# Banded attention and three dense stages on one core: chaining the attention's loads in twos, splitting queries and keys, and moving the first dense weights

## The chip, the cores and the metric

The kernel runs on one core of a Trainium2 chip. The metric is device time in microseconds (us). The median of three runs of the kernel before is 586.44 us.

Names in this text: PE is TensorE's matmul, PEld its weight load, DVE is VectorE, ACT is ScalarE, POOL is GpSimd, SP is SyncE, whose queue issues nearly all loads. A line number such as L353 is one of the kernel before.

## The reference, cut to what matters

```python
# attention: batch 2, 8 heads, 768 positions, head size 64; n_sink = 4, window = 128
scores = q @ k.T / 8
keep = (key position < n_sink) | (0 <= query position - key position < window)
a = exp(where(keep, scores, -1e9) - max);  a = a / (sum(a) + 1e-9)
x = (a @ v), heads side by side               # 1536 tokens x 512
# dense stages
h = ((x @ w1) * (x @ w2)) @ w3                # 512 -> 1024 -> 1024
x2 = h @ w_out                                # 1024 -> 512
g = softplus(x2 @ w_in2);  out = g @ w_out2   # 512 -> 2048 -> 512
```

The weights arrive in 64-bit floats, everything else in 32-bit floats.

## The kernel before, in words

**Attention.** The 16 pairs of batch and head are worked off as eight pairs of heads. For each pair, six tiles of 128 queries go through these steps: `S` (PE, `score`, L362: scores of a tile for both heads), `M` (DVE, `mask`: adds the mask and takes the extreme), `E` (ACT, `exp`), then for a whole head `N` and `RC` (DVE: total and reciprocal) and `C` (POOL, `divide`, L407), then `T` (PE, `turn`, L420: transposes), `P` (DVE or ACT: copies out of PSUM), `PV` (PE, `pv`, L441, in two banks: first the products with `v`, then those with `vu`, the sinks and the 64 keys before), and `XH`/`XL` (ACT and DVE: the result as a high and a low part).

**Loads.** A pair's queries and keys are one tile, `qk` (792 KB, `load_qk`, L351, one DMA; for the first pair four DMAs), its values are another with two DMAs, `v` and `vu` (384 and 400 KB, `load_v`, L355). There are two buffers of each tile, so the `qk` of a pair waits for the last scores of the pair two before, and its `v` for the last `PV` of the pair two before. All of these loads are issued by SP, in one order, and SP stands still while the one at the head of its queue waits.

**Order.** The order of all steps of the attention is written out by `Plan.order` (L96). Each step has an engine, a modelled duration, the steps that it comes after and a rank; the planner takes, again and again, the ready step with the least earliest start plus 0.9 times its rank. `add` (L477) makes the rank from the place in the program plus 45 times an entry of `PUT_OFF` (L50). The `after` of a load in the plan sets only its place in the order; what it really waits for follows from the buffers. Before, the plan puts the `v` of a pair behind the scores of its third tile.

**Dense weights.** A weight of 512 KB (128 partitions of 512 64-bit numbers) is loaded as 16-bit pieces into one of three `raw` buffers (L184) and decoded into a high and a low part by `decode_steps` (L178): two operations on ACT, three on DVE, then two more on POOL (inside the attention) or DVE, and a copy on ACT. The two halves of the first dense weight, `w12_0_0` and `w12_0_1`, are steps `D` of the attention's plan (L561 to L571): their loads stand behind the `v` of the fifth pair. The halves of the later weights are written behind the attention and are ordered by the framework. The first dense matmul reads the second half, `w12_0_1`.

**Dense stages.** They follow the attention on PE. Every product is three matmuls (`mm3`, L162: high by high, high by low, low by high). The decoded halves stand in a ring of five, the raw ones in three buffers.

Of the kernel before, what the change touches and what calls it, by code (L numbers as in the profile page):

```python
# [19 lines left out]

P = 128
B, H, S, D = 2, 8, 768, 64
NT = B * S
DM = 512
FF = 1024
FF2 = 2048
QT = S // P
NSINK = 4
U = 64
NU = S // U  # L30
KU = NSINK + U
KR = 80
EW = KU + P
NPAIR = H // 2
NC = DM // P
NF = FF // P
NF2 = FF2 // P
CH = 512
# [9 lines left out]


PUT_OFF = dict(  # L50
    nw=-0.5, iota=-300.95, iotb=-45.02, val=-247.3, inw=-311.11, cur=102.51, snk=-47.1, km0=104.75, m_0=-95.95,
    inb=-325.17, prev=40.33, m_p=159.53, m_c=-271.18, m_1=-154.82, heat=19.73, q0=(157.18, 60.63),
    k0=(253.67, 361.64), v=(-113.46, -289.26, -139.37, -113.46, -113.46, -342.06),
    S=(65.96, 59.23, -40.01, 65.96, 65.96, 63.13), M=(-188.89, -61.46, -238.48, -169.62, -188.52, -188.6),
    E=(51.48, 54.22, 37.52, 48.22, 49.01, 50.81), N=(-98.0, 45.02, -53.12, -11.42, 55.33, 31.4),
    RC=(-236.66, -396.73, -301.38, -324.52, -237.63, -429.07),
    C=(26.92, -265.71, 18.67, -185.09, 17.21, -231.23), T=(66.85, 66.45, 62.14, 58.83, 71.95, 61.32),
    P=(-672.43, -474.71, -617.58, -470.82, -715.87, -434.29), PV=(72.94, 71.29, 69.88, 72.94, 72.94, 86.56),
    XH=(-316.3, 47.28, -280.25, -316.3, -316.3, 24.42), XL=(64.31, 59.48, 59.9, 64.31, 64.31, 18.36),
    qk=(55.01, 50.02, 55.01, 55.01, 55.01, -46.54), flag=333.92, D=(61.63, 49.66),  # L60
)

PVS = (
# [5 lines left out]
class Plan:  # L69
# [6 lines left out]
        DMA=dict(DVE=2000, ACT=2000, Pool=2000, PE=2000, DMA=0),  # L76
# [7 lines left out]
    @staticmethod  # L84
    def form(s):
        return {"S": "quarters", "PV": "columns"}.get(s["key"][0], "whole")

# [52 lines left out]
class Net:  # L140
# [192 lines left out]
    def attention(self, pool, psum):  # L333
        nc = self.nc
# [2 lines left out]

        bufs = dict(qk=2, v=2, e=4, st=4, pt=4)
        shape = dict(qk=[P, S + NU * KU], v=[P, QT + NU - 2, P], e=[P, QT, EW], st=[P, 3, QT], pt=[P, 2 * QT - 1, P])
        users = {}  # L340

        def buf(tag, h):

            if (tag, h) not in held:
                held[tag, h] = pool.tile(shape[tag], F32, tag=tag, name=f"{tag}{h}", bufs=bufs[tag])
            return held[tag, h]

        def free(tag, h):
            return users.get((tag, h - bufs[tag]), [])

        def load_qk(pair, cuts=((0, S + NU * KU),)):  # L351
            for a, b in cuts:
                nc.sync.dma_start(out=buf("qk", pair)[:, a:b], in_=self.qk[pair][:, a:b])  # L353

        def load_v(pair):  # L355
            nc.sync.dma_start(out=buf("v", pair)[:, 0:QT], in_=self.v[pair])
            nc.sync.dma_start(out=buf("v", pair)[0:KR, QT:], in_=self.vu[pair])

        def tile_columns(i):
            return slice(KU, EW) if i == 0 else slice(0, EW)  # L360
# [61 lines left out]
        def on_dve(h, g):  # L422

            return g == 2 or g == 1 and h % 2 == 0
# [52 lines left out]
        def add(kind, engine, ns, emit, *args, after=(), ring=None, off=0):  # L477

            put, at = PUT_OFF.get(kind, 0), list(args)
            if at and kind not in ("heat", "q0", "k0", "D"):  # L480
                ends = (B * NPAIR, kind in ("S", "PV", "XH", "XL", "qk", "v"))
                last = ends[0] - 1 if ends[1] else 2 * ends[0] - 2
                at[0] = at[0] % 2 + (2 if at[0] < (1 if ends[1] else 2) else 4 if at[0] >= last else 0)
            while type(put) is tuple:
                put = put[at.pop(0)]
            rank = len(plan.steps) + off + 45 * put
            plan.add((kind, *args), engine, ns, lambda: emit(*args), after, rank, ring)
# [11 lines left out]
        heat = psum.tile([P, CH], F32, tag="X0", name="heat", bufs=1)  # L499
# [11 lines left out]
        for j in range(2):  # L511
            q, k = hq[j], slice(S + hc[j].start, S + hc[j].stop)
            last = [("k0", 0)] if j else []
            add("q0", "DMA", 1200 if j else 700, lambda j, q=q: load_qk(0, [(q.start, q.stop)]), j, after=last)
            add("k0", "DMA", 1300 if j else 730, lambda j, k=k: load_qk(0, [(k.start, k.stop)]), j, after=[("q0", j)])

        scores = [(pair, i) for pair in range(H * B // 2) for i in range(QT)]
        for pair in range(B * H // 2):
            heads = (2 * pair, 2 * pair + 1)
            if pair:  # L520

                add("qk", "DMA", 2900 if pair > 1 else 3300, load_qk, pair, after=free("qk", pair) + [("v", 0) if pair > 1 else ("k0", 1)])
            add("v", "DMA", 2900, load_v, pair, after=free("v", pair) + [("S", pair, 2) if pair else ("qk", 1)])
            for i in range(QT):
                n = scores.index((pair, i))
                need = [("qk", pair)] if pair else [(x, j) for x in ("q0", "k0") for j in range(1 + (i > 2))]
                need += [("S", *scores[n - 1])] if n else [("heat", j) for j in range(38)]
                need += [("heat", j) for j in range(38 if n == 3 else 48, 48 if n == 3 else 64)] if n in (3, 6) else []
                need += [("M", 2 * scores[n - 2][0] + par, scores[n - 2][1]) for par in range(2)] if n > 1 else []
                add("S", "PE", 346 if i else 200, score, pair, i, after=need)  # L530
                m = [] if pair else [(x,) for x in (("m_0",), ("m_1",), ("m_p",))[min(i, 2)]]
                for h in heads:
                    add("M", "DVE", 283 if i else 212, mask, h, i, after=[("S", pair, i), *free("e", h), *m])
                    add("E", "ACT", 442 if i else 385, exp, h, i, after=[("M", h, i)])
            users["qk", pair] = [("S", pair, i) for i in range(QT)]
            for h in heads:
                add("N", "DVE", 78, total, h, after=[("E", h, i) for i in range(QT)])
                add("RC", "DVE", 104, inverse, h, after=[("N", h)])
                for i in range(QT):
                    add("C", "Pool", 403 if i else 346, divide, h, i, after=[("RC", h)])  # L540
            for h in heads:
                for g in range(3):
                    need = [("C", h, 2 * g), ("C", h, 2 * g + 1)]
                    add("T", "PE", 440 if g else 330, turn, h, g, after=need, ring=("PT", ("P", h, g)))
                    to = ("DVE", 602) if on_dve(h, g) else ("ACT", 480 if g else 375)
                    add("P", *to, turned, h, g, after=[("T", h, g), *free("pt", h)])
                users["e", h] = [("T", h, g) for g in range(3)]
            for bank in range(2):
                need = [("P", h, g) for h in heads for g in ((2,) if bank else (0, 1))] + [("v", pair)]
                need += [("XL", pair - 1, bank)] if pair else []  # L550
                add("PV", "PE", 853 if bank else 1493, pv, pair, bank, after=need)
            users["v", pair] = [("PV", pair, b) for b in range(2)]
            for h in heads:
                users["pt", h] = users["v", pair]
            for bank in range(2):
                n = S - CH if bank else CH
                add("XH", "ACT", 50 + 0.84 * n, x_hi, pair, bank, after=[("PV", pair, bank)])
                add("XL", "DVE", 61 + 1.055 * n, x_lo, pair, bank, after=[("XH", pair, bank)])
            if pair == 1:
                h = 3  # L560
                add("flag", "DVE", 780, lambda: self.window_flag(pool), after=[("val",)], off=6)  # L561
                self.first = [
                    self.ring.tile([P, 2, CH], FR, tag="u", name=f"u_w12_0_{j}", bufs=5) for j in range(2)
                ]
                for j, u in enumerate(self.first):
                    need = [("v", 4)]
                    for k, (engine, ns, emit) in enumerate(
                        self.decode_steps(self.w12[0][:, j, :], u[:, 0, :], u[:, 1, :], f"w12_0_{j}", pool_too=True)
                    ):
                        add("D", engine, ns, lambda j, k, emit=emit: emit(), j, k, after=need)  # L570
                        need = [("D", j, k)]  # L571

        for s in plan.order(dict(PE=600, DVE=500, ACT=2000, Pool=500, DMA=1700)):
# [394 lines left out]
```

## Time and profile before

| | us |
|---|---|
| runs | 586.44, 589.6, 586.17 |
| median of the runs | 586.44 |
| profiled execution | 587.49 |
| its span, first to last instruction | 585.2 |
| mean granted clock of TensorE | 0.994 |
| first dense matmul | 77.92 from the span's start |
| data loaded and stored | 54.51 MB, mean 93 GB/s |

The page gives for each engine the busy time, its share of the span and the number of instructions. [...] The waits view and the brackets of the timeline name what ended an idle time; "issue" there is an idle time that ended without any event that the profile shows. The DMA view lists the packets of each queue in a stretch: q1 holds the loads, q8 and q14 the code of the engines.

### The profile page before, as it was taken

The page shows a single profiled execution, that of the slowest core. Times are in us where ns is not written, and L with a number is a line of the kernel's source. Part 1 is how long each engine was busy: PE and PEld are TensorE (multiplying, and loading weights), DVE is VectorE, ACT ScalarE, POOL GpSimd, SP SyncE. Part 2 cuts the span into 40 slices and gives each one's busy share as a digit, 9 for nine tenths or more (in the row PEclk, how much of TensorE's full clock was granted, in tenths as well). Part 3 has the DMA queues.
Part 4 walks back from the last instruction along what each step waited for, and adds up shares of the span by engine and source line. Part 5 has one row for each costly group of instructions (what it writes and reads, how often), then busy time and mean ns, then how long its engine had stood idle before and what let it go on. Part 6 is the DMA issues. An engine that isn't in the chain of part 4 may idle for free.

```text
span 585.2 us, 9853 instructions
## 1 busy us (share of the span) xinstructions
PE 575.0 (98%) x3728; PEld 475.5 (81%) x3728; DVE 432.0 (74%) x906; ACT 348.0 (59%) x712; POOL 77.2 (13%) x162
## 2 busy tenths in 40 slices
PE   8999899999999999999999999999999999999996
PEld 7788788888888788888888788888888888888885
DVE  6889699989998976775998899845644544654553
ACT  6899877667665664554566778544444344444352
POOL 3566620000000000000000110110110111011010
PEclk9999899999999999999999999999999999999998
DMA  7759434545543542441644031000200000200002
GB/s 234 212 179 266 150 111 151 146 134 161 159 148 109 155 134 72 144 143 37 183 143 141 21 124 38 0 1 0 73 0 2 1 2 0 73 0 1 0 1 78
DMA packets 15800, 54.51 MB, mean 93 GB/s; under 512 B 1920, under 2 KB 2432, under 8 KB 15744
## 3 DMA queue, kind: packets, MB, share of 16 engines
q1 hardware_dynamic: 15456, 53.27, 29.5%
q8 instruction: 31, 0.51, 0.4%
q10 hardware_dynamic: 288, 0.52, 0.2%
q14 instruction: 25, 0.20, 0.1%
HBM read 50.64 MB, written 3.15 MB: 92 GB/s over the span
## 4 chain that ended last, share of the span: by engine, by line
PE 64%; DMA 4%; DVE 4%; ACT 3%; issue 0%; POOL 0%; ACTq 0%; SPq 0%; DVEq 0%
PE h L166 7%; PE h L164 7%; PE h L165 7%; PE ox L164 4%; PE ox L166 4%; PE o L166 4%; PE x2p L164 4%; PE x2p L165 4%; PE o L164 4%; PE o L165 4%; PE ox L165 4%; PE x2p L166 4%; PE ab L166 3%; PE ab L165 3%; PE ab L164 3%; DMA raw_w<-w3t 3%
## 5 line engine op out<-in xcount | busy, mean ns | idle before, releaser
L709 POOL TENSOR_SCALAR spu<-spa 128x512 f32<-128x512 f32 (+1 forms) x49 | 30.7, 626 | 462.9 <-ACT spa L708 462.9
L149 DVE TENSOR_TENSOR gl<-spl,gh 128x512 fp32r<-128x512 f32 x47 | 32.7, 696 | 76.8 <-ACT gh L723 76.6
L707 ACT ACTIVATE spa<-h 128x512 f32<-128x512 f32 (+1 forms) x49 | 28.8, 587 | 88.4 <-PE h L166 88.2
L166 PE MATMUL ab<-x,u_w 128*128 128x512 f32 x192 | 74.8, 390 | 0.3 <-DVE u_w L149 0.3
L164 PE MATMUL ab<-x,u_w 128*128 128x512 f32 x192 | 74.8, 390 | 0.0
L165 PE MATMUL ab<-x,u_w 128*128 128x512 f32 x192 | 74.7, 389 | 0.0
L164 PE MATMUL h<-y,w4h 128*128 128x512 f32 x192 | 74.7, 389 | 0.0
L166 PE MATMUL h<-y,w4l 128*128 128x512 f32 x192 | 74.7, 389 | 0.0
L165 PE MATMUL h<-y,w4h 128*128 128x512 f32 x192 | 74.7, 389 | 0.0
L191 ACT ACTIVATE dt_w<-raw_w 128x512 bf16<-128x512 bf16 x64 | 42.4, 669 | 52.2 <-DVE dr_w L208 11.2
L199 DVE SCALAR_TENSOR_TENSOR dc_w<-raw_w,dt_w 128x512 uint16<-128x512 uint16 x64 | 44.5, 701 | 10.8 <-ACT dt_w L194 9.7
L194 ACT ACTIVATE dt_w<-dt_w,rebias 128x512 uint16<-128x512 uint16 x64 | 45.8, 722 | 1.4
L714 DVE SCALAR_TENSOR_TENSOR spu<-spu,spa 128x512 f32<-128x512 f32 (+1 forms) x49 | 33.3, 680 | 17.5 <-ACT spl L712 17.4
L393 ACT ACTIVATE e<-e,st 128x196 f32<-128x196 f32 (+1 forms) x96 | 42.2, 446 | 1.9 <-DVE st L386 1.9
L407 POOL TENSOR_SCALAR e<-e,st 128x196 f32<-128x196 f32 (+1 forms) x96 | 39.7, 437 | 26.6 <-ACT e L393 15.5
L166 PEld LDWEIGHTS ab<-x,u_w 128*128 128x128 f32 x192 | 36.0, 188 | 8.2 <-DVE u_w L149 0.7
L164 PEld LDWEIGHTS ab<-x,u_w 128*128 128x128 f32 x192 | 36.0, 188 | 7.6
L165 PEld LDWEIGHTS h<-y,w4h 128*128 128x128 f32 x192 | 36.1, 188 | 7.6
L166 PEld LDWEIGHTS h<-y,w4l 128*128 128x128 f32 x192 | 36.0, 188 | 7.5
L164 PEld LDWEIGHTS h<-y,w4h 128*128 128x128 f32 x192 | 36.0, 188 | 7.4
L165 PEld LDWEIGHTS ab<-x,u_w 128*128 128x128 f32 x192 | 36.0, 188 | 7.3
L712 ACT ACTIVATE spl<-spu 128x512 f32<-128x512 f32 (+1 forms) x49 | 30.5, 624 | 19.2 <-POOL spu L709 18.5
(127 smaller groups left out, 1311.3 us busy)
## 6 DMA issues: line engine op xcount, KB each, us to landing
raw_w<-w4d SPq DMA_DIRECT2D x32, 511.8 KB, 4.1
raw_w<-w SPq DMA_DIRECT2D x16, 511.8 KB, 4.5
raw_w<-w3t SPq DMA_DIRECT2D x16, 511.8 KB, 3.8
qk<-qk SPq DMA_DIRECT2D x7, 792.0 KB, 6.1
raw_wo<-wod SPq DMA_DIRECT2D x8, 511.8 KB, 3.7
v<-vu SPq DMA_DIRECT2D x8, 400.0 KB, 6.5
v<-v SPq DMA_DIRECT2D x8, 384.0 KB, 5.3
out<-os SPq DMA_DIRECT2D x10, 256.0 KB, 2.2
```

Of the source, the lines that this page charges most:

```text
L149: return engine.tensor_tensor(out=lo, in0=x, in1=hi.bitcast(F32), op=ALU.subtract)
L164: nc.tensor.matmul(ps, lhs[0], rhs[0], start=start, stop=False)
L165: nc.tensor.matmul(ps, lhs[0], rhs[1], start=False, stop=False)
L166: nc.tensor.matmul(ps, lhs[1], rhs[0], start=False, stop=stop)
L191: return nc.scalar.activation(t.bitcast(BF), x["top"].bitcast(BF), AF.Abs)
L194: return nc.scalar.activation(x["t"], x["t"], AF.Relu, bias=self.rebias[:, 0:1], scale=8.0)
L199: nc.vector.scalar_tensor_tensor(out=c, in0=x["top"], scalar=0x8000, in1=t, op0=ALU.bitwise_and, op1=ALU.bitwise_or)
L393: nc.scalar.activation(e, e, AF.Exp, bias=st[:, 0, i : i + 1], scale=-1.0, accum_out=st[:, 1, i : i + 1])
L407: nc.gpsimd.tensor_scalar(out=e, in0=e, scalar1=buf("st", h)[:, 2, i : i + 1], scalar2=1.0, op0=ALU.mult, op1=ALU.mult)
L709: nc.gpsimd.tensor_scalar(out=u[:, c], in0=a[:, c], scalar1=1.0, scalar2=1.0, op0=ALU.add, op1=ALU.mult)
L712: nc.scalar.activation(l[:, c], u[:, c], AF.Ln)
L714: nc.vector.scalar_tensor_tensor(out=u[:, c], in0=u[:, c], scalar=1.0, in1=a[:, c], op0=ALU.subtract, op1=ALU.subtract)
```

## The change

Each load of the attention's pairs, from the third pair on, and the load of each of the two first dense halves gets a dependence on the load issued two places before it in the list `loads`, with a real wait (`DependencyClass.Sync`). The loads of the first two pairs go on the list without a wait. `qk` of the pairs after the first is cut into queries (384 KB) and keys (408 KB), two DMAs. In the plan, a `v` comes after the scores of its pair's first tile (second pair: after the third pair's `qk`), the two dense halves come after the `v` of the third and of the fourth pair in place of the fifth, and loads are modelled with 3300 ns. All entries of `PUT_OFF` are new.

```diff
@@ PUT_OFF
-    nw=-0.5, iota=-300.95, iotb=-45.02, val=-247.3, inw=-311.11, cur=102.51, ...
+    nw=-0.5, iota=-317.65, iotb=-43.77, val=-256.36, inw=-267.68, cur=70.88, ...
...
-    qk=(55.01, 50.02, 55.01, 55.01, 55.01, -46.54), flag=333.92, D=(61.63, 49.66),
+    qk=(-10.74, -6.13, -10.74, -10.74, -10.74, -96.08), flag=262.31, D=(60.89, 63.1),
@@ attention
-        users = {}
+        users, loads = {}, []
...
-        def load_qk(pair, cuts=((0, S + NU * KU),)):
+        def behind(load, pair):
+            if pair > 1:
+                self.tc.add_manual_dep(
+                    load.ins, loads[-2].ins.name,
+                    mybir.DependencyInfo(mybir.DependencyClass.Sync, mybir.DependencyReason.DATA), reason="two loads",
+                )
+            loads.append(load)
+
+        def load_qk(pair, cuts=((0, S), (S, S + NU * KU))):
             for a, b in cuts:
-                nc.sync.dma_start(out=buf("qk", pair)[:, a:b], in_=self.qk[pair][:, a:b])
+                behind(nc.sync.dma_start(out=buf("qk", pair)[:, a:b], in_=self.qk[pair][:, a:b]), pair)
 
         def load_v(pair):
-            nc.sync.dma_start(out=buf("v", pair)[:, 0:QT], in_=self.v[pair])
-            nc.sync.dma_start(out=buf("v", pair)[0:KR, QT:], in_=self.vu[pair])
+            behind(nc.sync.dma_start(out=buf("v", pair)[:, 0:QT], in_=self.v[pair]), pair)
+            behind(nc.sync.dma_start(out=buf("v", pair)[0:KR, QT:], in_=self.vu[pair]), pair)
...
-                add("qk", "DMA", 2900 if pair > 1 else 3300, load_qk, pair, after=free("qk", pair) + [("v", 0) if pair > 1 else ("k0", 1)])
-            add("v", "DMA", 2900, load_v, pair, after=free("v", pair) + [("S", pair, 2) if pair else ("qk", 1)])
+                add("qk", "DMA", 3300, load_qk, pair, after=free("qk", pair) + [("v", 0) if pair > 1 else ("k0", 1)])
+            add("v", "DMA", 3300, load_v, pair, after=free("v", pair) + [("S", pair, 0) if pair > 1 else ("qk", pair + 1)])
...
-                    need = [("v", 4)]
+                    need = [("v", 2 + j)]
...
-                        add("D", engine, ns, lambda j, k, emit=emit: emit(), j, k, after=need)
+                        add("D", engine, ns, lambda j, k, emit=emit: behind(emit(), 2) if k == 0 else emit(), j, k, after=need)
```

## Rows read from the trace of the kernel before

**Rows 1.** The page, part 1: busy us, share of the span, instructions.
```profile
PE 575.0 (98%) x3728; PEld 475.5 (81%) x3728; DVE 432.0 (74%) x906; ACT 348.0 (59%) x712; POOL 77.2 (13%) x162
```

**Rows 2.** Windows: stretch, length, PE PEld DVE ACT POOL busy, PEclk, DMA share, GB/s.
```profile
16.00:18.00 2.00, 1.43 (x35) 1.05 (x36) 1.97 (x9) 2.00 (x11) 0.67 (x2) 1.00 0.89 219
...
60.00:62.00 2.00, 0.47 (x12) 0.38 (x14) 0.82 (x6) 0.94 (x6) 2.00 (x6) 1.00 1.02 397
...
63.10:66.50 3.40, 3.40 (x42) 2.61 (x41) 2.69 (x16) 2.72 (x12) 0.70 (x2) 0.50 0.04 12
...
sum 80.00, PE 75.54 PEld 63.10 DVE 63.91 ACT 67.36 POOL 46.58; mean PE 1.89 PEld 1.58 DVE 1.60 ACT 1.68 POOL 1.16
```

**Rows 3.** Timeline of PE: start us, us, what, count, idle before and its end.
```profile
17.11 0.79 PE L379 MATMUL s<-qk 64*64 64x128 f32 x24 [0.57 <-DMA qk<-qk]
...
31.37 0.79 PE L379 MATMUL s<-qk 64*64 64x128 f32 x24
...
45.47 0.90 PE L379 MATMUL s<-qk 64*64 64x68 f32 x32
...
58.40 1.62 PE L456 MATMUL xt<-pt,v 128*64 128x64 f32 x37
61.55 0.45 PE L456 MATMUL xt<-pt,v 68*64 68x64 f32 x7 [1.53 <-issue]
...
64.19 1.58 PE L379 MATMUL s<-qk 64*64 64x68 f32 x32
...
77.92 0.50 PE L164 MATMUL ab<-x,u_w 128*128 128x512 f32 x1
```

**Rows 4.** Waits: engine, line, releaser, us in total, times, longest.
```profile
PE xt L456 <- issue: 1.7, 2, 1.5
...
PE s L507 <- DVE idle L914: 1.0, 1, 1.0
...
PEld pt L420 <- issue: 1.6, 8, 0.3
```

**Rows 5.** Windows between the two "issue" waits; the page's instruction queue.
```profile
20.40:61.50 41.10, 39.55 (x886) 33.14 (x886) 36.16 (x169) 38.41 (x152) 26.70 (x62) 1.00 0.76 223
...
q8 instruction: 31, 0.51, 0.4%
```

**Rows 6.** DMA queues, 53.9 to 58.9 and 58.9 to 60.3: packets, MB, share.
```profile
q1 hardware_dynamic: 366, 1.27, 101.6%
...
q8 instruction: 1, 0.02, 5.4%
```

**Rows 7.** Timeline of SP's queue: start us, us, line, load, count.
```profile
24.58 6.36 SPq L353 DMA_DIRECT2D qk<-qk  x2
...
52.72 0.33 SPq L356 DMA_DIRECT2D v<-v  x1
...
53.57 1.38 SPq L187 DMA_DIRECT2D raw_w<-w  x3
```

**Rows 8.** Issues from 24.5, 34, 53.9, 74 us: count, KB each, us to landing.
```profile
qk<-qk SPq DMA_DIRECT2D x1, 792.0 KB, 5.6
...
v<-v SPq DMA_DIRECT2D x1, 384.0 KB, 3.4
...
raw_w<-w SPq DMA_DIRECT2D x3, 511.8 KB, 9.0
...
raw_wo<-wod SPq DMA_DIRECT2D x1, 511.8 KB, 3.7
```

**Rows 9.** Timeline of DVE, decode of the second dense half.
```profile
72.41 0.81 DVE L199 SCALAR_TENSOR_TENSOR dc_w<-raw_w,dt_w 128x512 uint16<-128x512 uint16 x1
...
73.70 0.79 DVE L208 SCALAR_TENSOR_TENSOR dr_w<-raw_w,dt_w 128x512 f32<-128x512 uint32 x1
```

**Rows 10.** Dense stage, 78 to 204 us: window, and PE's only wait there.
```profile
78.00:204.00 126.00, 125.82 (x554) 103.79 (x554) 117.45 (x221) 84.09 (x144) 0.00 (x0) 1.00 0.46 141
...
PE ab L166 <- DVE u_w L149: 0.3, 1, 0.3
```

More of the change, by code (lines that the diff above doesn't have):

```diff
@@ L50 @@
 PUT_OFF = dict(
[L51 to L59, printed above, removed]
-    qk=(55.01, 50.02, 55.01, 55.01, 55.01, -46.54), flag=333.92, D=(61.63, 49.66),
+    nw=-0.5, iota=-317.65, iotb=-43.77, val=-256.36, inw=-267.68, cur=70.88, snk=-194.23, km0=13.82, m_0=-40.84,
+    inb=-272.77, prev=42.97, m_p=72.04, m_c=-258.34, m_1=-102.89, heat=29.6, q0=(95.24, 95.41),
+    k0=(198.35, 341.02), v=(-254.09, -273.51, -124.74, -254.09, -254.09, -315.44),
+    S=(78.14, 70.61, -90.97, 78.14, 78.14, 72.39), M=(-126.74, 0.02, -182.88, -137.85, -183.95, -184.15),
+    E=(57.87, 58.44, -44.22, 57.55, 57.69, 61.31), N=(-232.84, -113.11, -108.47, -70.53, -51.12, -82.6),
+    RC=(-49.11, -236.6, -182.17, -214.72, -83.93, -241.17), C=(22.8, -309.04, 28.65, -135.73, 32.93, -305.93),
+    T=(76.97, 74.12, 72.61, 67.98, 80.4, 79.23), P=(-715.08, -387.66, -481.84, -445.05, -588.27, -305.45),
+    PV=(83.23, 86.96, 82.61, 83.23, 83.23, 92.27), XH=(-268.48, 58.65, -320.52, -268.48, -268.48, 125.99),
+    XL=(70.77, 69.43, 83.14, 70.77, 70.77, 68.26), qk=(-10.74, -6.13, -10.74, -10.74, -10.74, -96.08),
+    flag=262.31, D=(60.89, 63.1),
 )
```

## Prediction

> **What bounds the kernel now.** I read the page first. PE is busy for 98% of the span [rows 1], so a change of loads can only pay where PE stands still or runs at its low clock. [...] At 17.11 the scores of the third pair start 0.57 us late, on a `qk` load. At 61.55 the second product of the sixth pair (`pv`) goes on after 1.53 us idle, ended by "issue": nothing that the profile names released it. The list of waits has 1.7 us of that kind on PE, in two waits, and eight short ones, 1.6 us in all, on the weight loads of the turns [rows 4].
>
> What is "issue" here? The stall lies inside one `pv`: 37 of its 44 matmuls run, then 7 after the stall, so no new tile starts there. The counts give the place. From the "issue" wait at 20.4 us to that of 61.5 us, PE took in 886 matmuls and 886 weight loads, 1,772 instructions, and semaphore instructions that the view leaves out [rows 5]. The page has an instruction queue with 31 packets and 0.51 MB: 16.5 KB a packet, and 7,456 matmuls and weight loads divided by 31 are 240 a packet [rows 1, 5]. 1,772 is about seven of these (253 each). I read this as seven blocks of code, with both stalls at the seam of a block. The DMA view says when the block came: from 53.9 to 58.9 us the data queue takes 101.6% of the 16 engines and no instruction packet is among its 366; the next one comes between 58.9 and 60.3 [rows 6]. What filled the queue is on SP's timeline: `v` and `vu` of the seventh pair at 52.72, and three dense loads from 53.57 [rows 7], which took 9.0 us to land where one alone takes 3.7 [rows 8]. So PE ran out of code because its next block stood behind the loads in flight, and the fall of the clock followed the stall.
>
> [...]
>
> **The change part by part.**
> 1. *Each load of pairs 2 to 7, and the two first dense halves, wait for the load two places ahead.* At most two chained loads are then in flight, about 0.8 to 0.9 MB, where the four of 53 us and those before them put over 2 MB in front of a code block. Removed: the idle 1.53 us. Bounds: 0 (stall kept) and 1.7 (both PE waits of this kind). I take 1.5, since even one 792 KB `qk` alone in flight has left at most 0.3 us waits on the weight loads [rows 4].
> 2. *The low clock after the stall.* 3.4 us at half clock do 1.7 us of work [rows 2]; 32 score matmuls took 1.58 us there against 0.90 at 45.47 [rows 3]. If the stall goes, 1.7 us go; the 0.57 us stall at 17 us was followed by no fall (1.00 in its window). Bounds 0 and 1.7; I take 1.7.
> 3. *The wait itself, on SP's queue.* Behind a waiting load stand all later loads, and PE waits for these. Two in flight, each landing in 3.4 us like a `v` alone [rows 8], give one load every 1.7 us, so 6.8 us for the four of a pair; the pairs follow each other every 7.1 us (scores of the third at 17.11, of the fifth at 31.37 [rows 3]). It just fits. The pair that also carries a dense half needs 3.7 / 2 = 1.9 us more, 8.7 us, and lags by up to 1.6. The `qk` of the fifth pair was issued at 24.58 and landed 5.6 us later, 1.2 us ahead of its use [rows 3, 7, 8]. Bounds 0 and +1.6; I take 0, nearest to a pair without a dense half, of which there are more.
> 4. *`qk` in two loads.* Seven more issues on SP of about 0.4 us (0.33 us each on its timeline), in a queue that mostly waits. At the third pair, where `qk` was already 0.57 us late [rows 3], its first half now waits for the `v` of the first pair, but no longer shares with the loads behind it. Bounds −0.6 and +0.7 (as much again); I take 0.
> [...]
> 5. *The dense halves earlier.* The second half's decode stood in the tail: its two long VectorE operations at 72.41 and 73.70 [rows 9], followed by GpSimd's, just ahead of the first dense matmul at 77.92 that reads it. Had only the stall gone, that decode would have been the next thing late. Moved up, its 1.6 us of VectorE lie beside the middle pairs. Cost there: between 0 and 1.6; I take 0, since VectorE's score work waits for PE.
> 6. *The new weights of the planner* reorder steps on all engines; the trace cannot show the new order. PE's idle time in the first 80 us other than its first wait (1.0) and the stall is 1.9 us (80 less 75.5 busy, less 2.5 [rows 2, 4]), so a better order gives 1.9 at most; I allow the same as a loss and take 0.
> 7. *Hand-over.* From 78 to 204 us PE is busy 125.8 of 126, VectorE 117.5, and PE waits once, 0.3 us, for a decoded weight [rows 10]. The dense stage thus has no spare on either side. Bounds: all of the gain passes, or none. I take all: VectorE and ScalarE leave the attention earlier by the same 3.2 us, and VectorE has 1.6 us less to do in its tail.
>
> Sum: −1.5 − 1.7 = −3.2 us. The profiled execution took 587.49 us around a span of 585.2, 1.05 above the median of 586.44; its sum is 584.3, and against the median I predict **583.2**.
>
> **Rivals.**
> *The stall stays or comes back elsewhere.* Only chained loads wait. The two dense loads that stood right behind the second half at 53.57 (three in one row [rows 7]) are outside the attention and not chained; if they follow its new place at once, four loads of 0.4 to 0.5 MB are again in flight among the turns. For it: they were issued within 1.4 us of the first. Against: two chained loads beside them, not four. Half the stall and no fall of the clock gives 585; all of it 586.4. Centre 585.8. The stall also stays, at 586.4, if its cause is no missing code. [...]
> *Given back at 204 us.* If the decode chain does not move, PE's one wait grows from 0.3 to 3.5 us [rows 10] and the time is 586.4; half gives 584.8. For it: VectorE at 93%. Against: point 7.
> *A `qk` load late, on the slower side.* Place: fifth pair, 31.37. If the first dense half stands ahead of this `qk`, it is issued at about 24.6, and the second half of `qk` waits for it to land. Landing in 3.7 us gives 24.6 + 3.7 + 3.4 = 31.7, 0.3 us late. Beyond 31.37 every microsecond is PE's. With 7.4 us (between 3.7 alone and 9.0 in company [rows 8]) PE idles 4.0 us and then runs at half clock, another 1.7: −3.2 + 5.7 = +2.5, about 589. At 9.0 us it is +4.1, 590.5. It ends slower than before if the dense half takes more than 4.9 us to land: `qk` is then 1.5 us late, as long as the stall that the fall of the clock followed, and 1.5 + 1.7 eat the 3.2. Against: the chain keeps company small.
>
> **How the numbers follow.** Forecast 0.55 (581.3 to 585.1: a gain of 3.2 that points 3 to 6 move by 1.9 either way), stall back 0.13, given back 0.17, `qk` late 0.15. From 581.2 to 587.6 the range takes in the forecast, both middle rivals, and the mild end of the last. About 1%, 5.9 us, is what a measurement can tell from no change: faster than 580.6 needs nearly all idle time of the attention besides, 0.05; slower than 592.3 needs two late loads, 0.04; within, 0.91.
>
> **What would show it.** Right: no "issue" wait of over 0.5 us on PE before the dense stage; the clock at 1.00 from 60 to 70 us; the first dense matmul at about 74.7 instead of 77.92; PE's wait near 201 us not over 0.5. Wrong: an idle stretch of PE ended by a `qk` load (the third rival); an instruction packet again missing from a long stretch of full queue (the first); a first dense matmul that is early with a wait of microseconds near 200 us (the second).

## The result, and the profile after

| | before | after |
|---|---|---|
| median, us (6 runs each) | 585.79 | 592.3 |
| lowest to highest, us | 583.44 to 589.6 | 591.12 to 592.82 |
| ratio, 95% interval | 1 | 1.0109 (1.0073 to 1.0145) |
| profiled execution, its span, us | 587.49, 585.2 | 592.09, 589.3 |
| mean granted clock | 0.994 | 0.993 |
| first dense matmul of the unbroken dense stage, us | 77.92 | 83.00 |

The changed kernel is slower by 6.4 us (4.3 to 8.5); I had predicted 583.2 and at most 587.6. Its code stands a few lines lower: `score` is L387, `turn` L428, `pv` L464, the loads of `qk`, `v` and `vu` L361, L364 and L365; the dense load keeps L187. Everything in this section is of the changed kernel.

The page has the same work as before [rows 1]:

```profile
PE 575.5 (98%) x3728; PEld 475.9 (81%) x3728; DVE 431.3 (73%) x906; ACT 348.6 (59%) x712; POOL 76.2 (13%) x162
```

The windows answer [rows 2, 10] (columns as there; the stretches come from several answers):

```profile
50.00:52.00 2.00, 0.00 (x0) 0.00 (x0) 0.44 (x3) 2.00 (x9) 1.09 (x3) 0.95 0.37 138
52.00:54.00 2.00, 0.23 (x4) 0.26 (x8) 0.00 (x0) 1.04 (x6) 1.30 (x4) 0.50 0.19 68
...
51.81:58.63 6.82, 4.86 (x60) 4.14 (x62) 2.98 (x11) 1.23 (x6) 1.49 (x4) 0.50 0.59 180
...
sum 82.00, PE 73.75 PEld 61.04 DVE 61.30 ACT 66.22 POOL 45.92; mean PE 1.80 PEld 1.49 DVE 1.50 ACT 1.62 POOL 1.12
...
83.00:209.00 126.00, 126.00 (x560) 104.34 (x557) 119.81 (x225) 85.52 (x144) 0.00 (x0) 1.00 0.45 147
```

From 60 to 62 us nothing stands still any more. In its place PE does nothing from 50 to 52 us and little from 52 to 54, and its granted clock is 0.50 from 51.8 to 58.6; 1.00 and 0.50 are the only two levels in this trace and in that of the kernel before. The timeline and the waits of PE (columns as in [rows 3, 4]) give the names:

```profile
13.64 0.49 PE L387 MATMUL s<-qk 64*64 64x68 f32 x9 [0.49 <-issue]
...
16.88 0.79 PE L387 MATMUL s<-qk 64*64 64x128 f32 x24 [0.34 <-DMA qk<-qk]
...
21.08 0.57 PE L464 MATMUL xt<-pt,v 68*64 68x64 f32 x11 [1.06 <-issue]
...
32.40 0.79 PE L387 MATMUL s<-qk 64*64 64x128 f32 x24
...
53.77 1.36 PE L387 MATMUL s<-qk 64*64 64x128 f32 x24 [4.49 <-DMA qk<-qk]
...
65.85 2.73 PE L464 MATMUL xt<-pt,v 128*64 128x64 f32 x72
...
83.00 0.50 PE L164 MATMUL ab<-x,u_w 128*128 128x512 f32 x1
```

```profile
PE s L387 <- DMA qk<-qk: 4.8, 2, 4.5
PE xt L464 <- issue: 1.1, 1, 1.1
...
PE s L387 <- issue: 0.5, 1, 0.5
```

The scores of the seventh pair wait 4.49 us for `qk`. The bank of 72 matmuls at 65.85 runs whole, where before one was cut by the stall. But two stalls that end with "issue", 0.49 and 1.06 us, have come at 13.64 and 21.08.

Why was that `qk` late? The chain of waits, read backwards from 53.77 (start us, us, what), leads through three loads, the second and the third each held by the one before:

```profile
36.85 4.52 DMA v<-v
...
41.38 3.79 DMA raw_w<-w
...
45.19 8.44 DMA qk<-qk
...
53.77 1.36 PE s L387 x24
```

The first of them was held too: by the waits of SP's queue it stood 1.8 us for the first half of the sixth pair's `qk`, two places ahead, and went at 36.85.

And SP's queue shows what stood between them (as [rows 7]); below it the landing times of those issues (as [rows 8]):

```profile
36.85 0.33 SPq L364 DMA_DIRECT2D v<-v  x1
37.83 0.33 SPq L365 DMA_DIRECT2D v<-vu  x1
41.38 1.96 SPq L187 DMA_DIRECT2D raw_w<-w  x3
43.44 2.08 SPq L361 DMA_DIRECT2D qk<-qk  x2
```

```profile
raw_w<-w SPq DMA_DIRECT2D x3, 511.8 KB, 7.4
qk<-qk SPq DMA_DIRECT2D x1, 408.0 KB, 8.4
...
qk<-qk SPq DMA_DIRECT2D x1, 384.0 KB, 9.2
```

The row of three dense loads is the point. The first is the second dense half, which the chain holds until the fourth pair's `v` has landed at 41.37. The other two belong to the second dense weight: they are written behind the attention, carry no wait, and the framework has put them right behind the half, as before [rows 7]. There they came after nearly all loads of the attention; now the `qk` of the seventh pair stands behind them. Its first half is issued at 43.44, its second waits for the dense half and goes at 45.19, and they take 9.2 and 8.4 us to land.

**The accounting of the profiled execution.** PE idles 82 − 73.75 = 8.25 us in its first 82, against 80 − 75.54 = 4.46 in 80 before [rows 2]: +3.8. The low clock does 4.86 us of work, at half speed a loss of 2.4, against 1.7 before: +0.7. In the dense stage PE waits for nothing, where it waited 0.3 [rows 10]: −0.3. Sum +4.2; the span grew by 4.1. The medians differ by more, 6.5 us, because the profiled execution of the kernel before stands 1.7 us above its median and that of the changed kernel 0.2 us under its own. Nor does the low clock come in every execution: the run of 591.12 us had a mean clock of 0.999, too high for 6.8 us at half clock.

### The profile page after: what moved, and what is told of

It reads as the page before. It is cut to its first block, busy times and chain, and to the rows that moved or that the text cites. A ratio compares the mean times of both kernels' runs of the same rounds, so it can differ in the third digit from the quotient of the medians.

```text
span 589.3 us, 9869 instructions
## 1 busy us (share of the span) xinstructions
PE 575.5 (98%) x3728; PEld 475.9 (81%) x3728; DVE 431.3 (73%) x906; ACT 348.6 (59%) x712; POOL 76.2 (13%) x162
## 4 chain that ended last, share of the span: by engine, by line
PE 91%; DMA 5%; ACT 1%; POOL 1%; SPq 1%; issue 0%; DVE 0%; POOLq 0%
PE ab L164 7%; PE ab L165 7%; PE ab L166 7%; PE h L166 7%; PE h L165 7%; PE h L164 7%; PE ox L164 4%; PE ox L166 4%; PE o L166 4%; PE x2p L165 4%; PE x2p L164 4%; PE ox L165 4%; PE o L165 4%; PE o L164 4%; PE x2p L166 4%; PE xt L464 3%
```

## Experiments

Three theories were put to the test. **A**: the two unchained dense loads in front of the seventh `qk` make it late. **B**: the chain itself does, by its waits. **C**: something else in the change, such as its new order. Ratios are to the kernel before, on the same chip; "hold" means that the two loads of the second dense weight are ordered behind the attention's last load. The first pair of runs, with the result and the eighth, makes a table of two by two:

| | the two dense loads ahead of `qk` | held behind the attention |
|---|---|---|
| chain | the change: 1.0109 (1.0073 to 1.0145) | `hold_next`: 1.0024 (1.0000 to 1.0049) |
| no chain | `no_chain`: 1.0011 (0.9986 to 1.0035) | `hold_no_chain`: 0.9975 (0.9955 to 0.9996) |

**hold_next**: the change, with the hold.

```diff
+            if k == 0 and name.startswith("w12_1_"):
+                self.order(self.last_load, done)     # an order on SP's queue, no semaphore
@@ behind
+            self.last_load = load
```

> The changed kernel, but the two loads of the second dense weight may not be ordered ahead of the attention's last load. Theory A (three dense loads, one chained and two not, stand ahead of the seventh pair's queries and keys on SP's queue and in the DMA engines): the wait of 4.5 us at that pair's scores falls under 1 us, the clock stays at 1.00 from 48 to 60 us, and the time falls by 4.5 and the 2.3 that the low clock cost, to about 585.5 (584 to 587.5). Theory B (the wait for the load two places ahead makes queries and keys late by itself): the chain is untouched, so the wait stays above 3 us and the time above 590. Theory C (the planner's new weights order the steps worse): above 590 too, without a long wait being needed.

586.15 us, ratio 1.0024. As A expected. SP's queue, and the landing of the same `qk`:

```profile
43.38 2.81 SPq L364 DMA_DIRECT2D qk<-qk  x2
```

```profile
qk<-qk SPq DMA_DIRECT2D x1, 408.0 KB, 3.8
...
qk<-qk SPq DMA_DIRECT2D x1, 384.0 KB, 4.1
```

The first half is issued at 43.38, within 0.06 us of the changed kernel's 43.44, and lands in 4.1 us in place of 9.2. The scores of the seventh pair no longer wait, and the clock is 1.00 from 48 to 60 us (24 scores in 0.79 us at 50.19, against 1.36 in the changed kernel). What the chain still costs is on PE's timeline:

```profile
32.74 0.86 PE L390 MATMUL s<-qk 64*64 64x128 f32 x24 [1.43 <-DVE st L414]
...
38.37 0.84 PE L431 MATMUL pt<-ident,e 128*128 128x128 f32 x3 [0.64 <-POOL e L418]
...
50.19 0.79 PE L390 MATMUL s<-qk 64*64 64x128 f32 x24
```

The view names DVE for the 1.43 us, but the second half of this `qk` landed at 32.60, just before the scores start: it is the load.

**no_chain**: the change with the dependence switched off (`if pair > 99` in `behind`), the dense loads where they are.

> The changed kernel without the waits for the load two places ahead; order and splitting as in the changed kernel. Theory A: the three dense loads still stand ahead of the seventh pair's queries and keys, but are issued some 3 us earlier, so that pair still waits 1 to 3 us: 587 to 590. Theory B: no wait at that pair, 584 to 586. Theory C: 591 to 593, as the order of the steps is unchanged. If missing code was the cause of the stalls ended by nothing, they are as long as before or longer here.

585.37 us, ratio 1.0011: A missed, and what B expected came. The profiled execution was the slowest of its runs (588.56). In it the seventh `qk` is no wait at all, though the same three dense loads stand ahead of it:

```profile
35.95 1.84 SPq L187 DMA_DIRECT2D raw_w<-w  x3
...
40.29 0.81 SPq L361 DMA_DIRECT2D qk<-qk  x2
```

```profile
qk<-qk SPq DMA_DIRECT2D x1, 408.0 KB, 7.3
...
qk<-qk SPq DMA_DIRECT2D x1, 384.0 KB, 5.9
```

It lands slowly here too (5.9 and 7.3 us), but it was issued at 40.29, three microseconds earlier, and so is in time for 48.61. B fails by hold_next, where the chain is untouched. So neither A nor B stands alone: the chain delays the issue, the dense loads lengthen the landing, and `qk` had room for one of the two. And without the chain the stalls ended by nothing are still there, one followed by the low clock:

```profile
14.64 0.49 PE L387 MATMUL s<-qk 64*64 64x68 f32 x9 [1.37 <-issue]
...
48.61 0.79 PE L387 MATMUL s<-qk 64*64 64x128 f32 x24
...
51.38 1.17 PE L428 MATMUL pt<-ident,e 128*128 128x128 f32 x7 [1.75 <-issue]
```

```profile
14.63:51.38 36.75, 34.39 (x757) 28.05 (x757) 30.99 (x148) 34.34 (x129) 24.03 (x56) 1.00 0.78 245
...
52.05:55.46 3.41, 3.41 (x45) 3.08 (x45) 2.72 (x9) 0.94 (x5) 0.37 (x1) 0.50 0.07 16
```

Between them lie 757 matmuls and 757 weight loads, 1,514 in all. With PE's semaphore instructions, which the views leave out, the trace has 1,536 = 6 × 256.

**one_qk**: the change with `qk` in one load.

> The changed kernel with a pair's queries and keys in one load of 792 KB as before, chained. Theories A, B and C alike: no cause lies in the splitting itself, 590 to 594. If two small loads are what makes them late: back by over 3 us, under 589.

586.22 us, 1.0025 (1.0001 to 1.0050): all theories missed but the aside that small loads are what makes it late. Counting two places back in a list with one entry less, the `qk` no longer hangs on the dense half, and the fourth pair's `v` no longer on a half of the sixth pair's `qk`. That `v` goes at 34.38 in place of 36.85, the three dense loads at 38.20 in place of 41.38, and the `qk` at 40.98; it lands in 8.4 us as well. PE waits, and the clock holds (24 scores in 0.79 us right after the wait, against 1.36 in the changed kernel):

```profile
49.51 0.79 PE L387 MATMUL s<-qk 64*64 64x128 f32 x24 [1.70 <-DMA qk<-qk]
```

So the halves cost by what they wait for, not by their size.

**dense_late**: the change with both dense halves back behind the fifth pair's `v` (`need = [("v", 4)]`).

> The changed kernel with both first dense halves again ordered behind the fifth pair's values. Their loads then stand behind the seventh and eighth pair's queries and keys, chain and splitting unchanged. Theory A: no wait over 1 us at the seventh pair, about 585.5 (584 to 588; a stall on missing code near 60 us may come back). Theory B: still above 590 with a long wait on queries and keys. Theory C: above 590.

587.10 us, 1.0049 (1.0027 to 1.0071), inside A's range; the profiled execution was the slowest (588.85). The dense loads come at 55.26 and PE's waits for `qk` shrink to 0.2 us, as A would have it; but others come, the longest on POOL, and "issue" waits of 0.8 and 0.4 us:

```profile
69.70 0.81 PE L428 MATMUL pt<-ident,e 128*128 128x128 f32 x3 [1.22 <-POOL e L415]
```

**before_hold**: the kernel before, with the hold; does the stall at 60 us go when two loads of the three of 53.6 us are taken away?

> The kernel before, with one edit: the two loads of the second dense weight may not be ordered ahead of the attention's last load. Theory of the code block (PE's next block of instructions waits behind the loads in flight): with two loads of 512 KB fewer near 54 us the wait ended by nothing near 60 us shrinks from 1.5 us to under 0.7, the clock does not fall there, and the executions that had it are 3 us shorter: median 0.5 to 2 us under the kernel before, with less spread. If the block does not wait behind loads: the stall stays, 584 to 586. If the second dense weight then comes too late for the dense stage: a wait of PE on a decoded weight appears after 78 us, slower by 1 to 3 us.

586.17 us, 1.0011 (0.9986 to 1.0037). It does not:

```profile
58.37 1.62 PE L458 MATMUL xt<-pt,v 128*64 128x64 f32 x37
61.60 0.45 PE L458 MATMUL xt<-pt,v 68*64 68x64 f32 x7 [1.60 <-issue]
```

The stall has the same place and length (1.60 against 1.53 [rows 3]) with only one dense load behind `v`. So the two loads that I had counted in do not make it. The packet of q8 ahead of the stall's end begins at 58.92 here and at 58.98 in the kernel before; whether it stands behind the loads that are left, issued up to 53.21, was not tested.

**before_chain**: the kernel before, with the chain alone.

> The kernel before with the waits for the load two places ahead alone; one load for queries and keys, dense halves, durations and planner weights as before. Theory A (the long wait needs the chain and the unchained dense loads directly ahead of a pair's queries and keys): here the dense loads follow the last queries and keys, so no wait over 1.7 us; the chain still delays single loads, 584.5 to 587. Theory B (the chain alone does it): above 589.

585.68 us, 1.0006 (0.9981 to 1.0030). The stall at 60 us is gone, and the gain is spent elsewhere: the first dense half is issued at 47.38 in place of 43.09, ACT waits for it, and PE's second product of `x` waits behind that, with 3.4 us at 0.50 after it:

```profile
52.61 0.66 ACT L191 ACTIVATE dt_w<-raw_w 128x512 bf16<-128x512 bf16 x1 [2.40 <-DMA raw_w<-w]
```

```profile
54.04 1.75 PE L464 MATMUL xt<-pt,v 128*64 128x64 f32 x28 [2.21 <-DVE x L149]
```

B, which wanted over 589, fails: in the old order the chain alone makes no difference that these runs can tell.

**d_free**: the change, with the dense halves' own loads unchained (`behind(emit(), 0)`).

> The changed kernel, in which the loads of the two first dense halves do not wait for the load two places ahead; all else chained as in the changed kernel, the order of SP's queue the same. Theory A with its refinement (the chain held the second dense half until the values ahead had landed, at 41.4 us, and so put three dense loads right before the seventh pair's queries and keys): the dense loads go out some 3 us earlier, the wait of 4.5 us shrinks to 1 to 2 us and the clock holds, 586 to 588.5. If only the dense traffic counts and not when it starts: 591 to 593 again.

589.42 us, 1.0067 (1.0037 to 1.0097), a microsecond above the range that A expected. The `qk` is issued at 42.46, lands in 5.9 us, and PE waits 0.41:

```profile
49.48 0.79 PE L387 MATMUL s<-qk 64*64 64x128 f32 x24 [0.41 <-DMA qk<-qk]
```

The profiled execution was the fastest of its runs (586.89), so it shows how the wait goes but not where its median loses; that stays open.

**hold_no_chain**: the change with both delays removed.

> The changed kernel with neither the chain nor the second dense weight's loads ahead of the attention's last load. Theory A: no wait on queries and keys; what is left against the kernel before is the order of the steps and waits on missing code, 583 to 586. Theory C (the new order of the steps is worse by itself): 586 to 588 although no load is late.

584.56 us, 0.9975 (0.9955 to 0.9996): faster than both kernels, as A expected. The window of the first 78 us, in this kernel, in the changed one and in the one before:

```profile
0.00:78.00 78.00, 76.24 (x1538) 63.33 (x1539) 64.95 (x304) 68.73 (x252) 46.31 (x113) 1.00 0.69 208
```

```profile
0.00:78.00 78.00, 69.80 (x1435) 57.73 (x1436) 58.93 (x286) 62.52 (x239) 44.62 (x110) 0.96 0.66 202
```

```profile
0.00:78.00 78.00, 73.54 (x1521) 61.45 (x1521) 62.04 (x290) 66.21 (x245) 46.58 (x113) 0.98 0.67 202
```

PE idles 1.8 us here, 8.2 in the changed kernel, 4.5 before, and the clock holds at 1.00. That C, which puts the loss on something else in the change, is not needed follows from it: without the two delays the rest of the change gains.

**hold_no_chain_2**: the same kernel again, in five rounds.

> The changed kernel with neither the chain nor the second dense weight's loads ahead of the attention's last load, measured again in more rounds: 0.2 to 0.4% under the kernel before, interval below 1.

584.87 us, 0.9977 (0.9955 to 0.9999). The waits of PE in the whole span:

```profile
PE s L518 <- DVE idle L925: 1.0, 1, 1.0
PE pt L431 <- ACT pt L443: 0.2, 1, 0.2
```

**hold_three**: the hold, and the chain of two widened to three (`loads[-3]`).

> The changed kernel with the second dense weight's loads behind the attention's last load, and each chained load waiting for the load three places ahead in place of two. Theory A (the chain costs by issuing loads late): between the chain of two (ratio 1.0024) and no chain (0.9975), about 584.5 to 586 if the kernel before is at 585. If a chain also spares waits on missing code worth more than it costs: below the kernel without a chain.

584.83 us, 0.9985 (0.9965 to 1.0006); beside the start PE waits once for 0.3 us and once for 0.2. A third load in flight removes what the chain of two cost; more than no chain it does not give.

**seam_shift**: the kernel before, without the last 16 of the 64 matmuls of zeros in `warm` (L507); nothing reads these 16. They stand behind the sixth score tile, so all that follows has 32 PE instructions fewer ahead of it. If the stall at 61.55 is at the seam of a block of code, it comes 32 instructions later in the program.

> The kernel before without the last 16 of its 64 warm-up matmuls (after the sixth score tile), which leaves PE's later program the same but 32 instructions shorter ahead of it. Theory of the code block: the seam between two blocks moves 16 matmuls later in the program. The wait ended by nothing, which stood after 37 of the 44 matmuls of the sixth pair's first product, now stands after all 44 and 9 of the score matmuls that follow; the one near 20 us, after 61 of 72, stands after all 72 and 5 transposes. If the wait belongs to a tile, a semaphore or a load: it stays after 37 of 44. Time within 2 us of the kernel before.

587.87 us, 1.0036 (1.0013 to 1.0060), 2.03 us above the kernel before where at most 2 were expected. The stall has moved to exactly there:

```profile
55.24 0.43 PE L379 MATMUL s<-qk 64*64 64x128 f32 x3 [0.54 <-issue]
...
59.03 1.81 PE L456 MATMUL xt<-pt,v 128*64 128x64 f32 x44
60.77 0.44 PE L379 MATMUL s<-qk 64*64 64x68 f32 x9
...
62.03 0.78 PE L379 MATMUL s<-qk 64*64 64x128 f32 x23 [0.82 <-issue]
```

It followed 37 of the 44 matmuls of this product [rows 3]; now it follows 44 and 9 score matmuls, 16 later. It follows the count of instructions, not the work. The other stall, 0.2 us at 20.43 before, did not move along: PE passes its new place without a wait. In its stead one of 0.54 us stands at 55.24, and from there to 62.03 PE's instructions, semaphores included, are 256 again.

**old_weights**: `hold_no_chain` with the old `PUT_OFF`, to separate the new order from the new places.

> The kernel with neither chain nor early second dense weight, but with the planner's weights of the kernel before; durations, places and splitting of the changed kernel. If the new weights are what gains on the kernel before: 1 to 3 us slower than with the new weights, ratio 0.999 to 1.003. If holding the dense loads and splitting gain by themselves: ratio 0.996 to 0.999, as with the new weights.

595.51 us, 1.0181 (1.0154 to 1.0209): both expectations missed. With the dense halves in their new places the old weights put the first dense matmuls among the turns, and PE waits for a weight that ACT has not decoded, with the clock at 0.50 from 68.07 to 74.90:

```profile
68.73 0.79 PE L164 MATMUL ab<-x,u_w 128*128 128x512 f32 x1 [2.06 <-ACT u_w L224]
```

The weights belong to the places; what each is worth alone this run cannot say.

**The four corners.** In us of 585.8 they are +6.4, +1.4, +0.6 and −1.5. From the last one the chain alone costs 2.9 and the dense loads alone 2.1, in sum 5.0; together 7.9. That taking either out of the changed kernel helps is resolved. That the two are worth more together, 2.9 us, is not resolved by the times: the four half-widths, 0.0036, 0.0025, 0.0024 and 0.0021, add in quadrature to 0.0054, or 3.2 us. It is the traces that show it: 4.49 us of idle PE on this `qk` with both, none with either alone.

## Why the prediction was wrong

It failed at **step 3**, the wait on SP's queue, which I took as 0 with an upper bound of +1.6. It measured 4.49 us of idle PE, and a low clock of 2.4 after it.

1. *The stall goes, −1.5.* The one at 61.55 went. Two of 0.49 and 1.06 came at 13.64 and 21.08, 1.55 in sum against 1.7 before [rows 4]. So this term was about 0. That a stall of this kind stands at a fixed count of PE's instructions was right: with 32 fewer ahead of it, it came 16 matmuls later (seam_shift). The two stalls before, which I had counted about seven blocks of 253 apart, are 1,792 = 7 × 256 instructions apart when PE's semaphore instructions are counted too. That the chain prevents such a stall is not shown: 0.4 us of "issue" was left in the old order (before_chain), 1.55 in the new. That a block of code stood behind the loads in flight was an estimate of mine that no run shows: before_hold took two of them away, and the stall was 1.60 us against 1.53. In the new order the three kernels with the hold have 0.3 us of it at most, with the chain or without. Yet in the chained kernels the hold moves no load ahead of 41 us, and two of these stalls lay at 13.64 and 21.08; why they are missing there is open, with one profiled execution of each.
2. *The low clock goes, −1.7.* It went with that stall, and a longer one came with the idle time ahead of 53.77 us (0.50 for 6.8 us in place of 3.4).
3. *The wait.* "At most two in flight" counted only the chained loads, and 3.4 us was the landing of a load with little company [rows 8]. With two more loads that no chain governs ahead of it, the `qk` took 9.2, and it went late because the chain had first held the dense half, and with it everything behind it on SP, until 41.37. My bound of +1.6 allowed for one dense half in the chain and for nothing behind it.
4. *`qk` in two loads.* At the third pair I was right that little would change: 0.34 us in place of 0.57. What I did not see is that a half more shifts what "two places ahead" means: the second half hung on the dense half (one_qk).
5. *The dense halves earlier.* In hold_no_chain they cost PE nothing. Their place mattered by what came along, the two loads behind them. I did price that, in the rival of the returning stall, but as a block of code held up by them (at most 586.4), not as a load of the attention behind them in the queue.
6. *The new weights.* Bounded by ±1.9, taken as 0. With both delays removed, PE's idle time in the first 78 us falls from 4.5 to 1.8 and the time by 1.5 us (hold_no_chain). That is the new order, the new places, the split and the hold together; what the weights alone are worth stays open (old_weights).
7. *The hand-over.* Right, in the other direction: the first unbroken dense matmul came 5.1 us later, of which 0.46 us of dense work had been done before it and 0.3 us of a later wait vanished, and the span grew by 4.1. The rival "given back at 204 us" did not occur.

The rival that came true is **a `qk` load late**, given 0.15. Its mechanism was right to the part (a dense half ahead of `qk`, the second half waiting for it, a landing of up to 9.0 us, then the half clock) and so was its price (4.0 idle and 1.7 of clock for a landing of 7.4; it was 4.49 and 2.4). I put it at the fifth pair, where the scores now start at 32.40 without a wait; it was the seventh. "The chain keeps company small" was the argument against, and it is the sentence that the trace refutes. With the measured figures its sum, −3.2 + 4.49 + 2.4, is +3.7, near the 4.1 us by which the span grew. The time was above its 589 to 590.5 in part because the 3.2 us had been read in one execution and were taken off the median, 1.05 us under that execution; how much of them a median execution had, one profile cannot say. The forecast has the same flaw.

Two smaller slips in the prediction's sums do not bear on this. "Half the stall and no fall of the clock" gives 584.0 by the terms of the sum, not 585. The loads at 53 us were five, not four [rows 7].

## What to carry to other kernels

A limit on loads in flight holds only if every load of that queue is under it, also those that another part of the program or the framework puts there: here two loads were outside it, and the first half of a `qk` landed in 9.2 us with them ahead and in 4.1 without. So before you chain loads, list what stands in the queue behind each chained one. With the chain this half was issued at 43.44 in place of 40.29 (no_chain), and with the two dense loads ahead it took 5.1 us longer to land; it had room for one and not for both, so test a wait and company together and apart. A stall that ends with nothing in the profile can be tested by a few instructions more or less ahead of it: the one of 1.53 us came 16 matmuls later in the program with 32 instructions fewer ahead of it, and so hung on their count and not on a tile or a load. And take a gain that was read in one profiled execution off that execution's time, not off the median.

## What the runs showed of the hardware

- **Landing was longer in company, and the tail was slow.** The same 384 KB, issued at 43.38 and 43.44, took 4.1 and 9.2 us, with one dense load just ahead and with three. From 50.8 to 53.4 us in the changed kernel the data queue used only a sixth of the 16 engines, 15.7% (packets, MB, share), and still the second half of the `qk` landed only at 53.63:

```profile
q1 hardware_dynamic: 56, 0.15, 15.7%
```

- **Stalls at multiples of 256 instructions.** The waits views of the fourteen traces have 17 waits of PE for "issue", 0.2 to 1.75 us long. Counted with the semaphore instructions from the start of each trace, all 17 come after 192 PE instructions and a whole multiple of 256 (after 448 and 704 in the changed kernel, 704 and 2,496 in the one before), also in seam_shift, where the same work has 32 instructions fewer ahead of it. In the traces of these two kernels q8 has 31 packets of 16,384 bytes, and the n-th of them begins ahead of the place at 192 + n × 256, for all 28 such places. Up to the dense stage PE never passed a place earlier than 2.2 us after its packet had begun, and the 17 waits ended 2.3 to 2.7 us after it began. That these stalls are waits for the packet is my reading of these times; no event in the profile says so, and what set the packet's start was not separated.
- **The clock around an idle stretch.** With 4.49 us of idle PE up to 53.77 the granted clock was 0.50 for 6.8 us, from 51.81 on, of which 4.86 were work; after 1.53 before and 1.75 in no_chain, for 3.4. It held after the 1.70 of one_qk (24 scores in 0.79 us), so in these traces the length of one idle stretch does not decide it alone.
